# Attention with a gated MLP on one core: 128-query units open their P.V later, their maxima are added by an identity matmul, and one chunk's output is made in two passes

## The chip, the cores and the metric

The kernel runs on one core of one Trainium2 chip. The metric is device time in microseconds (us) of one execution. The engines are PE (TensorE, with PEld for its weight loads), DVE (VectorE), ACT (ScalarE), POOL (GpSimd) and SP (SyncE, which here issues every DMA).

## The reference

The inputs are x [1, 2048, 512], wqkv [512, 1536], wo [512, 512], w1 and w3 [512, 1792], w2 [1792, 512], all bfloat16. Attention has 32 heads of 16 columns.

```python
xn = _layernorm(x)
qkv = (xn @ wqkv).reshape(B, S, 3, H, Dh).transpose(2, 0, 3, 1, 4)
scores = einsum("bhqd,bhkd->bhqk", q, k) * Dh ** -0.5
p = softmax(scores)
o = einsum("bhqk,bhkd->bhqd", p, v).transpose(0, 2, 1, 3).reshape(B, S, D) @ wo
h = silu(x @ w1) * (x @ w3)          # of xn
out = h @ w2
return x + o + out
```

Both branches read the same normalised x; the result is x plus attention plus MLP.

## The kernel before, in words

**Units.** Queries come in 4 chunks of 512 (`qc`), heads in 8 groups of 4 (`g`). A unit is one chunk, one head group and 256 queries; the first two units and the last 16 have 128 queries. There are 73 units, in order of chunk and then group.

**Scores twice.** For each unit the scores are made in two layouts. First with queries on partitions ("p1", L1022), two matmuls of 512 keys into two PSUM banks, which one DVE `tensor_reduce` turns into maxima (L1062, tile `part`): 1,024 of these in all, 16 for a unit of 256 queries and 8 for one of 128. Banks 0 to 3 serve p1, two at a time. Then with keys on partitions ("p2", L1286), one bank at a time out of banks 4 to 7, from which ACT writes exponentials into `PT` (L1299; L1329 does two banks in one instruction, a "pair"): 2,048 banks in all, 32 for a unit of 256 queries and 16 for one of 128. `PT` has 37 slots.

**Maxima into the scores.** The negated maximum of each query has to be in two extra rows of `QT` before p2 of the unit can begin ("AUG"). The final maximum is taken on DVE (L1199) for the first three and the last eight units and by six small POOL instructions for the others (L1170 to L1177); POOL then writes `Z` (L1147, L1149; DVE does it for the last unit). From `Z` there are two ways. In `FAST_AUG` units (the first three, the last eight) PE builds the unit's q afresh from `xnT` with padded weights, four matmuls (for the last two groups of heads with `wq_last`), adds the rows of `Z` through an identity matmul, and ACT moves the result into `QT` (tile "AQ", L797). In all other units SP issues a transposing DMA `Zs<-Z` (L1193) and two DMAs `QT<-Zs` (L1189).

**P.V.** When a unit has at most `PV_LEFT` = 6 exponentials missing, its P.V tile takes one of banks 4 to 7 (L569); ACT copies the result to `U` (L1394), and DMAs and POOL normalise it (L1419, L1439). The last three units (`FAST_PV`) are normalised on DVE instead: a reciprocal (L1384) and a product (L1386), in DVE's queue.

**The rest.** MLP pairs (56, G and U tiles) use the same four banks; ACT evacuates each pair three times (L838, L840, L844) and POOL makes `hT`, which has room for 24 pairs. The output of a chunk (OUT, 4 tiles, PE by the helper line L583, ACT L904) adds x, 14 matmuls with `hT` and 8 with the normalised attention. Its `hT` slots come free when it is done, and only then may later pairs start (`pred_g`). The last chunk has its MLP part first (OUTA, L921) and its attention part added on DVE (OUTB, L935).

**What sets the order.** A greedy planner writes the whole program ahead of time, engine by engine, from costs that it assumes. Every engine then runs its list strictly in order. PE is filled with work of no use ("fill", `xnT,ident` matmuls) where its recent columns fall under a bound:

```python
if recent_cols(c[0]) < RECENT_MIN and c[0] <= end + URG_WAIT:
    return c[0], c[3] if len(c) > 3 else c[1]
```

with 9,400 columns in 2.9 us before. An output is opened by this line, the P.V tile by the next two:

```python
if outs and n >= out_from(NT - 4 - len(outs)) and ok(outs[0]) and exp_unit[min(pv_u[0], NU - 1)] <= OUT_EXP:
left = len(p2_list[u]) - exp_unit[u]
if left > PV_LEFT:
```

Of the kernel before, what the change touches and what calls it, by code (L numbers as in the profile page):

```python
# [215 lines left out]

class _Tile:
# [15 lines left out]
def _c_act(n):  # L233
    return n / 1200.0 + 0.05
# [14 lines left out]
def _build(nc, A_x, A_wqkv, A_wo, B_w1, B_w3, B_w2, out):  # L249
# [12 lines left out]
    NPT = 37  # L262
    NKQ = 2
    NUB = 2
    TOL = 0.0
    PV_LEFT = 6
    ROW_LEAD = 0.45
    PAIR_WAIT = 0.05
    PAIR_DEPTH = 3
    COVER = 0.6  # L270
    MATE = 0.0
    TILE_BANKS = None
    A_LEAD = 0.7
    ROW_LEAD2 = 0.45
    LEAD_AT = 620
    RELAX = 0.06
    PACE = 4500
# [7 lines left out]
    UNIT_TAIL = {i: (128,) * 4 for i in range(1, 5)}  # L285
    DMA_FIRST = 2.95
    DMA_RATE = 360.0
    NFAST = 8
    NPADQ = 2
    NOW = 2  # L290
    WARM_FILL = 12.0
# [9 lines left out]
    OUT_EXP = 14  # L301
# [9 lines left out]
    LOAD_RATE = 5000.0  # L311
    LOAD_CAP = 3000.0
    LOAD_MIN = 3000.0
    RECENT = 2.9
    RECENT_MIN = 9400.0
    URG_WAIT = 0.12
    P2_LOOK = 8
    KEEP = 0.1
    COUPLE = 0.12
# [17 lines left out]
    N_FAST0 = 3  # L337
    FAST_AUG = set(range(N_FAST0)) | set(range(NU - NFAST, NU))
# [8 lines left out]
    with ctx:  # L347
# [18 lines left out]
        wq_last = sb("wq_last", [128, NPADQ, DC * 4 * 32], BF16)  # L366
# [103 lines left out]
        P.op("dve", lambda e: e.memset(wq_last[:, :, :], 0.0), writes=[("wq7",)], occ=0.3 * NPADQ)  # L470
# [60 lines left out]
        def pad(dst, src, g):  # L531
# [4 lines left out]
        padq = {g: wq_last[:, g - NG + NPADQ, :].rearrange("p (a d) -> p a d", d=32)  # L536
                for g in range(NG - NPADQ, NG)}
# [6 lines left out]
        for g in padq:  # L544
            dl, sl_ = pad(padq[g], wq[:, :, :], g)
            poolq["pad"].append(_Item(lambda e, dl=dl, sl_=sl_: e.tensor_scalar(dl, sl_, 1.0, 0.0, ALU.mult, ALU.add),
                                      [("wq",)], [("wq7",)], 0.4, pred=lambda: ("KT", 0, NQC - 1) in done))
        wpad = {("k", 0): wk_first, ("q", 0): wq_first}
        wpad.update({("q", g): padq[g] for g in padq})
# [219 lines left out]
        def qt_groups(qc, g, q0, nq, stop_last):  # L769
            groups = []  # L770
            for c in range(DC):
# [3 lines left out]
                    ([("wq7",)] if g else [("wq0",)] + ON0_KEYS) + xnT_keys(qc * 512 + q0, nq), _c_mm(nq), None))  # L775
# [10 lines left out]
        def tile_QT2(u):  # L786
# [3 lines left out]
            groups = qt_groups(qc, g, q0, nq, False)  # L790
# [20 lines left out]
        def ffn_pair(sc, fc):  # L811
# [35 lines left out]
            def pred_g():  # L847
# [10 lines left out]
                return all(("OUT", (idx - NHT) // FC * 4 + ts) in done for ts in range(4))  # L858
# [16 lines left out]
        def g_h(tg, fc, stop=False):  # L875
# [3 lines left out]
                                          start=False, stop=stop),  # L879
# [13 lines left out]
        def tile_OUT(tg):  # L893
# [4 lines left out]
            def evac(bk):  # L898
                def cb(op):
                    store(tg)  # L900
                    done.add(("OUT", tg))
                    if tg + NXR < NT:
                        load_xr(tg + NXR)
# [1025 lines left out]
```

## Time and profile before

| | us |
|---|---|
| median of 3 runs | 1203.73 |
| the three runs | 1202.17, 1203.73, 1207.64 |
| the profiled execution's own time | 1202.28 |
| its span, first to last instruction | 1200.4 |
| granted TensorE clock, mean | 0.996 |
| busy in the span: DVE / ACT / PE / POOL | 1181.3 / 1169.9 / 1124.1 / 439.3 |

All durations below come from the one profiled execution. Its time stands 1.88 us above its span. A duration on ACT is longer than the step from one instruction to the next, since neighbours overlap by about 0.1 us; steps are taken as the difference of two starts. Line numbers are those of the kernel before; in the kernel after the same statements have other numbers.

### The profile page before, as it was taken

What the parts mean: (1) busy time and instruction counts of PE and PEld (TensorE: products, weight loads), DVE (VectorE), ACT (ScalarE), POOL (GpSimd) and SP (SyncE); (2) the same over time, 40 slices, a digit from 0 to 9 for tenths busy, and PEclk for the clock granted to TensorE, in tenths of its full rate; (3) what the DMA queues carried; (4) which work ended last, traced back from release to release, by engine and by line L of the source; (5) the groups of instructions that cost most, each with busy time, mean ns of one, the idle gap of its engine ahead of it and who ended that gap; (6) DMA issues with size and microseconds to landing.
All of it is one profiled execution on the core that took longest, in us unless ns stands there. A gap on an engine that the chain in (4) does not pass through costs nothing.

```text
span 1200.4 us, 32683 instructions
## 1 busy us (share of the span) xinstructions
PE 1124.1 (94%) x13504; PEld 466.0 (39%) x13660; DVE 1181.3 (98%) x1088; ACT 1169.9 (97%) x2280; POOL 439.3 (37%) x856
## 2 busy tenths in 40 slices
PE   8999999999999999998999999998899999999997
PEld 3433333333334433343333333333333333445554
DVE  9999999999999999999999999999999999999995
ACT  7889999999999999999999999999999999999997
POOL 3254645625222255552222246652222125233220
PEclk9999999999999999998999999999999999999999
DMA  6423223221001121210001122210000111110000
GB/s 188 117 66 82 62 57 76 57 52 41 25 22 33 38 57 42 56 38 19 20 18 31 33 55 59 53 37 20 22 20 24 34 40 24 26 26 19 12 9 25
DMA packets 131248, 52.02 MB, mean 43 GB/s; under 512 B 100140, under 2 KB 131100, under 8 KB 131100
## 3 DMA queue, kind: packets, MB, share of 16 engines
q1 hardware_dynamic: 131100, 49.93, 16.6%
q8 instruction: 107, 1.75, 0.6%
q14 instruction: 41, 0.34, 0.1%
HBM read 38.86 MB, written 6.74 MB: 38 GB/s over the span
## 4 chain that ended last, share of the span: by engine, by line
ACT 38%; PE 34%; DVE 25%; issue 2%; DMA 0%; POOL 0%; ACTq 0%; another core or an unknown queue 0%
ACT PT L1299 29%; DVE part L1062 23%; PE ps L583 13%; PE ps L1286 10%; PE ps L569 6%; ACT PT L1329 5%; PE ps L1022 5%; ACT th L838 1%; ACT zg L840 1%; ACT U L1394 1%; ACT ub L844 1%; ACT kq L745 1%; DVE t L610 1%; DVE hT L643 0%; ACT Vaug L760 0%
## 5 line engine op out<-in xcount | busy, mean ns | idle before, releaser
L1062 DVE TENSOR_REDUCE part<-ps 128x2 f32<-128x1024 f32 x1024 | 1160.2, 1207 | 1.5 <-PE ps L1286 0.7
L1299 ACT ACTIVATE PT<-ps 128x512 bf16<-128x512 f32 x1800 | 944.5, 634 | 5.4 <-PE ps L1286 4.1
L1286 PE MATMUL ps<-QT,KT 32*128 32x256 bf16 (+1 forms) x4672 | 549.4, 259 | 9.9 <-ACT PT L1329 4.3
L1022 PE MATMUL ps<-KT,QT 32*128 32x512 bf16 x2048 | 403.1, 385 | 8.3 <-DVE part L1062 4.0
L1286 PEld LDWEIGHTS ps<-QT,KT 32*128 32x128 bf16 x4672 | 208.1, 92 | 230.2 <-issue 95.9
L1419 POOL TENSOR_TENSOR Rc<-Lc,mone 128x8 f32<-128x8 f32 (+1 forms) x70 | 105.8, 1512 | 268.0 <-DMA Lc<-U 267.9
L583 PE MATMUL ps<-xnT,ident 128*128 128x512 bf16 (+1 forms) x565 | 167.4, 350 | 25.0 <-ACT PT L1329 9.8
L569 PE MATMUL ps<-PT,Vaug 128*17 128x256 bf16 (+1 forms) x4672 | 185.0, 263 | 6.3 <-ACT PT L1299 1.8
L583 PE MATMUL ps<-xnT,w 128*128 128x512 bf16 (+1 forms) x538 | 145.9, 337 | 11.6 <-ACT zg L840 5.0
L1022 PEld LDWEIGHTS ps<-KT,QT 32*128 32x128 bf16 x2048 | 98.6, 91 | 129.9 <-DVE part L1062 73.2
L1329 ACT ACTIVATE PT<-ps 128x1024 bf16<-128x1024 f32 x124 | 127.0, 1056 | 1.7 <-PE ps L1286 1.6
L569 PEld LDWEIGHTS ps<-PT,Vaug 128*17 128x17 bf16 x4672 | 85.7, 89 | 92.0 <-issue 64.7
L583 PEld LDWEIGHTS ps<-xnT,ident 128*128 128x128 bf16 x652 | 48.1, 96 | 106.6 <-ACT PT L1299 54.2
L825 POOL TENSOR_TENSOR a<-zg,ub 128x512 f32<-128x512 bf16 x56 | 64.5, 1152 | 45.8 <-ACT ub L844 45.6
L583 PEld LDWEIGHTS ps<-xnT,w 128*128 128x128 bf16 x566 | 43.1, 97 | 80.4 <-issue 47.4
L827 POOL TENSOR_TENSOR hT<-a,t 128x512 bf16<-128x512 f32 x56 | 70.9, 1266 | 2.5
L583 PE MATMUL ps<-w,hT 128*128 128x256 bf16 (+1 forms) x266 | 68.3, 338 | 2.1 <-issue 1.3
L1170 POOL TENSOR_TENSOR mx<-part 128x16 f32<-128x16 f32 (+1 forms) x62 | 13.1, 211 | 152.6 <-DVE part L1062 152.5
L1439 POOL TENSOR_TENSOR wk_on<-U,R 128x256 bf16<-128x256 f32 (+1 forms) x37 | 23.3, 630 | 92.3 <-DMA R<-rd 92.3
L1439 POOL TENSOR_TENSOR on_b<-U,R 128x256 bf16<-128x256 f32 (+1 forms) x33 | 23.4, 709 | 81.6 <-DMA R<-rd 81.4
L822 POOL TENSOR_SCALAR t<-th 128x512 f32<-128x512 bf16 x56 | 34.7, 619 | 11.5 <-ACT th L838 9.4
L838 ACT ACTIVATE th<-ps 128x512 bf16<-128x512 f32 x56 | 36.0, 642 | 2.3 <-PE ps L583 2.3
(88 smaller groups left out, 509.8 us busy)
## 6 DMA issues: line engine op xcount, KB each, us to landing
w<-in_B_w_dram SPq DMA_DIRECT2D x112, 128.0 KB
R<-rd SPq DMA_DIRECT2D x55, 128.0 KB
QT<-qd SPq DMA_DIRECT2D x31, 128.0 KB
KT<-kd SPq DMA_DIRECT2D x28, 128.0 KB
xr<-in_A_x_dram SPq DMA_DIRECT2D x16, 128.0 KB
out_dram<-osb SPq DMA_DIRECT2D x16, 128.0 KB
qd<-kq SPq DMA_DIRECT2D x15, 128.0 KB
w<-in_B_w_dram SPq DMA_DIRECT2D x1, 1792.0 KB
```

The lines of the kernel that those rows point to most:

```text
L569: ins = e.matmul(bank(bk)[32 * i:32 * i + m, c0 + a:c0 + b], make_lhsT(i), rhs if (a, b) == (0, ncols) else rhs[:, a:b], start=start, stop ...
L583: return e.matmul(bank(bk)[0:rows, c0 + a:c0 + b], lhsT, rhs if (a, b) == (0, ncols) else rhs[:, a:b], start=start, stop=stop, **kw)
L825: q.append(_Item(lambda e: e.tensor_tensor(a32[:, :], zg[:, ss, :], ub[:, ss, :], ALU.mult), [("zg", ss), ("ub", ss)], [("a32",)], 1.1, 1.25))
L827: q.append(_Item(lambda e: e.tensor_tensor(hT[:, hslot(idx), :], a32[:, :], t1[:, :], ALU.mult), [("a32",), ("t1",)], [("hT", hslot(idx))] ...
L838: return [_Item(lambda e: e.activation(th[:, ss, :], bank(bk), ACTF.Tanh, scale=0.5), [("ps", bk)], [("th", ss)], _c_act(512), cb=part_don ...
L1022: ins = e.matmul(bank(2 * sl + i), QT[32 * j:32 * j + 32, qs, q * 128:(q + 1) * 128], KT[32 * j:32 * j + 32, g, c_ * 512:(c_ + 1) * 512], ...
L1062: redq.append(_Item(lambda e: e.tensor_reduce(dst, pair_ap.rearrange("p (a b) -> p a b", b=512), AX.X, ALU.max), writes, [("part", par, qt ...
L1286: ins = e.matmul(bank(b)[:, i * nq:(i + 1) * nq], KT[32 * j:32 * j + 32, g, (k0 + i) * 128:(k0 + i + 1) * 128], QT[32 * j:32 * j + 32, qs, ...
L1299: expq.append(_Item(lambda e: e.activation(PT[:, sl, :], bank(b), ACTF.Exp, scale=SCALE), [("ps", b)], [("PT", sl)], _c_act(512), cb=cb, e ...
L1329: return _Item(lambda e: e.activation(PT[:, s0:s1 + 1:s1 - s0, :], ps8[:, b0:b1 + 1, :], ACTF.Exp, scale=SCALE), [("ps", b0), ("ps", b1)], ...
L1419: poolq["nrm"].append(_Item(lambda e: e.tensor_tensor(Rc[:, pp, 0:nl], Lc[:, pp, 0:nl], mone[:, 0:nl], ALU.pow), [("Lc", pp), ("mone",)], ...
L1439: poolq["nrm"].append(_Item(lambda e: e.tensor_tensor(onorm[ob][:, g, q0:q0 + nq], U[:, us, 0:nq], R[:, pp, 0:nq], ALU.mult), [("U", us)] ...
```

## The change

Six things change together.

1. A unit of 128 queries opens its P.V when 2 exponentials are missing, not 6 (`PV_LEFT_S`).
2. An AQ tile no longer rebuilds q: one identity matmul copies the unit's columns of `QT`, and the rows of `Z` are added as before. So any unit can use it: `FAST_AUG` is now the first 8 units and the last 16. The final maximum stays on DVE for the same eleven units as before (`DVE_MAX`). `wq_last` and what filled it go, and `PT` has 39 slots.
3. The output of chunk 2 has two passes: OUTP makes its 14 `hT` matmuls as soon as its MLP pairs are done and leaves them in `osb`; OUT later adds x, `osb` (through the identity) and the 8 attention matmuls.
4. Later MLP pairs wait for the `hT` part of the earlier output ("HP") instead of the whole output.
5. The bound for fill is 12,800 columns in 3.413 us, of which the last 0.3 us are taken as 1,900 columns per us.
6. Two exponentials may be paired if their banks are neighbours, as before; the constants move into an object `K`, with the same values. `LEADS` is empty and `LEAD2` is 0, so they do nothing.

```diff
-    NPT = 37
+    NPT = 39
+    K = _Lead(ROW_LEAD=0.45, LEAD2=0.0, ANY_PAIR=0, A_LEAD=0.7, RELAX=0.06, KEEP=0.1, PAIR_WAIT=0.05, COVER=0.6, URG_WAIT=0.12, HORIZON=0.3, LOAD_RATE=5000.0, PV_LEFT=6, PV_LEFT_S=2, OUT_EXP=14, PACE=4500, MATE=0.0, COUPLE=0.12)
+    TWO_PASS = (2,)
+    LEADS = {}
...
-    RECENT = 2.9
-    RECENT_MIN = 9400.0
+    CLOCK_W = 3.413
+    CLOCK_MIN = 12800.0
+    ROW_RATE = 1900.0
...
-    FAST_AUG = set(range(N_FAST0)) | set(range(NU - NFAST, NU))
+    FAST_AUG = {u for u in range(NU) if u < FAST_HEAD or u_tr[u] >= FAST_TR}
+    DVE_MAX = {u for u in range(NU) if u < DVE_HEAD or u >= NU - DVE_TAIL}
...
-        P.op("dve", lambda e: e.memset(wq_last[:, :, :], 0.0), writes=[("wq7",)], occ=0.3 * NPADQ)
...
-            groups = qt_groups(qc, g, q0, nq, False)
+            groups = [(lambda bk: all_groups(bk, ident[:, :], QT[:, qs, q0:q0 + nq], nq, stop=False, skip=True),
+                       [("ident",)] + qh_keys(qs, q0, nq), _c_mm(nq), None)]
...
-                return all(("OUT", (idx - NHT) // FC * 4 + ts) in done for ts in range(4))
+                return all(("HP", (idx - NHT) // FC * 4 + ts) in done for ts in range(4))
...
-            groups = [g_x(tg)] + [g_h(tg, fc) for fc in range(FC)]
+            two = qc in TWO_PASS
+            groups = [g_x(tg)] + ([g_b(ts)] if two else [g_h(tg, fc) for fc in range(FC)])
...
+        def g_b(ts):
+            return (lambda bk: all_groups(bk, ident[:, :], osb[:, ts, :], D, start=False, stop=False),
+                    [("ident",), ("osb", ts)], _c_mm(512), None)
+
+        def tile_OUTP(tg):
+            qc, ts = divmod(tg, 4)
+            groups = [g_h(tg, fc, fc == FC - 1, fc == 0) for fc in range(FC)]
+
+            def evac(bk):
+                return [_Item(lambda e: e.activation(osb[:, ts, :], bank(bk), ACTF.Identity),
+                              [("ps", bk)], [("osb", ts)], _c_act(512), cb=lambda op: done.add(("HP", tg)))]
...
-            if u not in FAST_AUG:
+            if u not in DVE_MAX:
                 pool_max()
...
-            if left > PV_LEFT:
+            if left > (K.PV_LEFT if units[u][3] > 128 else K.PV_LEFT_S):
...
+            if parts and ok(parts[0]) and n >= PART_FROM[parts[0].name]:
+                return parts.pop(0)
...
-            if recent_cols(c[0]) < RECENT_MIN and c[0] <= end + URG_WAIT:
+            if recent_cols(c[0], CLOCK_W - K.HORIZON) + ROW_RATE * K.HORIZON < CLOCK_MIN and c[0] <= end + K.URG_WAIT:
```

Since the planner decides again with every one of these, the order moves all along the program. Counted over the whole of it, ACT has 50 single exponentials fewer and 25 pairs more, 8 AQ evacuations of 128 columns and 5 of 256 more, and 4 more copies into `osb`. SP has 39 DMAs fewer (13 transposes, 26 into `QT`). PE has 32 `wq_last` matmuls fewer, 8 of group 0 fewer, 24 of `QT` and 18 of `Z` more, and fill worth 40 more matmuls of 512 columns. DVE loses one memset, and has the following change of order at its end. The names are those of the groups above: `part` and `negm` are maxima, `R` and `wk_on` the reciprocal and normalised attention of the third last unit.

DVE before, from the second last unit's final maximum:

```order
L1199 TENSOR_REDUCE negm<-part 128x4
L1062 TENSOR_REDUCE part<-ps 128x2 x7
L1199 TENSOR_REDUCE negm<-part 128x4
L1147 TENSOR_SCALAR Z<-negm 128x4
L1149 TENSOR_TENSOR Z<-negm,Z 128x4
L1384 RECIPROCAL R<-ps 128x128
L1386 TENSOR_TENSOR wk_on<-ps,R 128x128
```

DVE after, at the same place:

```order
L1216 TENSOR_REDUCE negm<-part 128x4
L1079 TENSOR_REDUCE part<-ps 128x2 x6
L1401 RECIPROCAL R<-ps 128x128
L1403 TENSOR_TENSOR wk_on<-ps,R 128x128
L1079 TENSOR_REDUCE part<-ps 128x2
L1216 TENSOR_REDUCE negm<-part 128x4
L1164 TENSOR_SCALAR Z<-negm 128x4
L1166 TENSOR_TENSOR Z<-negm,Z 128x4
```

The reciprocal and the product of the third last unit have moved ahead of the last maximum of the last unit.

ACT before, from the AQ evacuation of the last unit (the row ahead of these) to the end:

```order
L1329 ACTIVATE PT<-ps 128x1024
L1299 ACTIVATE PT<-ps 128x512 x2
L1329 ACTIVATE PT<-ps 128x2x512
L1299 ACTIVATE PT<-ps 128x512 x2
L1329 ACTIVATE PT<-ps 128x2x512
L1299 ACTIVATE PT<-ps 128x512 x2
L1329 ACTIVATE PT<-ps 128x2x512
L1299 ACTIVATE PT<-ps 128x512 x3
L1329 ACTIVATE PT<-ps 128x2x512
L1299 ACTIVATE PT<-ps 128x512 x3
L1329 ACTIVATE PT<-ps 128x2x512 x2
L1299 ACTIVATE PT<-ps 128x512 x2
```

ACT after, from the same evacuation (its row included) to the end:

```order
L796 ACTIVATE QT<-ps 128x128
L1316 ACTIVATE PT<-ps 128x512
L1346 ACTIVATE PT<-ps 128x2x512
L1316 ACTIVATE PT<-ps 128x512 x2
L1346 ACTIVATE PT<-ps 128x2x512
L1316 ACTIVATE PT<-ps 128x512 x2
L1346 ACTIVATE PT<-ps 128x2x512
L1316 ACTIVATE PT<-ps 128x512 x2
L1346 ACTIVATE PT<-ps 128x2x512 x2
L1316 ACTIVATE PT<-ps 128x512 x2
L1346 ACTIVATE PT<-ps 128x2x512
L1316 ACTIVATE PT<-ps 128x512
```

Behind that evacuation stood 14 single exponentials and 7 pairs; now 10 singles and 6 pairs.

ACT before, behind the last output of chunk 2 (`osb`), with the MLP pairs of chunk 3 that had to wait for it:

```order
L904 ACTIVATE osb<-ps 128x512
L1299 ACTIVATE PT<-ps 128x512 x3
L838 ACTIVATE th<-ps 128x512
L840 ACTIVATE zg<-ps 128x512
L1329 ACTIVATE PT<-ps 128x2x512
L1299 ACTIVATE PT<-ps 128x512 x2
L844 ACTIVATE ub<-ps 128x512
L1299 ACTIVATE PT<-ps 128x512 x8
L1394 ACTIVATE U<-ps 128x256
```

ACT after, behind the same output (`t` is the first OUTA tile of chunk 3):

```order
L905 ACTIVATE osb<-ps 128x512
L1316 ACTIVATE PT<-ps 128x512 x14
L936 ACTIVATE t<-ps 128x512
L1316 ACTIVATE PT<-ps 128x512 x7
L1411 ACTIVATE U<-ps 128x256
L1316 ACTIVATE PT<-ps 128x512 x19
L936 ACTIVATE a<-ps 128x512
```

Four MLP pairs (12 evacuations) stood behind it, one of which is shown; now none does.

More of the change, by code (lines that the diff above doesn't have):

```diff
@@ L901, in cb @@
                     done.add(("OUT", tg))
+                    done.add(("HP", tg))
                     if tg + NXR < NT:
@@ L1624, in note_load, with recent_cols @@
             recent.append((st, w))
-        def recent_cols(st):
-            while recent and recent[0][0] < st - 4.0:
+        def recent_cols(st, span):
+            while recent and recent[0][0] < st - 5.0:
                 recent.pop(0)
-            return sum(w for t, w in recent if t >= st - RECENT)
+            return sum(w for t, w in recent if t >= st - span)
         def low_load(st):
@@ L1703, in pick_pe @@
             if a is not None:
-                late = P.free["dve"] + sum(it.occ for it in redq) - A_LEAD
+                late = P.free["dve"] + sum(it.occ for it in redq) - K.A_LEAD
                 rows.append((max(late, a[2]), a))
```

93 lines of the change are left out of this document (48 added, 45 removed).

## Prediction

> **What bounds the kernel now.** I read the page's busy times first, then the groups, then DVE's waits, then the chain.
>
> ```profile
> PE 1124.1 (94%) x13504; PEld 466.0 (39%) x13660; DVE 1181.3 (98%) x1088; ACT 1169.9 (97%) x2280; POOL 439.3 (37%) x856
> L1062 DVE TENSOR_REDUCE part<-ps 128x2 f32<-128x1024 f32 x1024 | 1160.2, 1207 | 1.5 <-PE ps L1286 0.7
> ```
>
> DVE and ACT are both nearly full. DVE's part is one thing: 1,024 maxima that take 1160.2 us, 1.133 us each, with 1.5 us of idle time ahead of them. The change takes none away, so the end of the maxima can come earlier by 1.5 us at most. DVE's waits for scores (engine, line, released by: total us, times, longest), and the stretches of time in which they lie:
>
> ```profile
> DVE part L1062 <- PE ps L1286: 0.7, 2, 0.5
> DVE part L1062 <- PE ps L1022: 0.6, 1, 0.6
> ...
> 557.00:560.40 3.40, 2.38 (x24) 0.82 (x19) 3.40 (x4) 3.40 (x5) 0.21 (x1) 1.00 0.09 24
> 560.40:563.80 3.40, 2.99 (x35) 0.90 (x39) 3.16 (x4) 2.97 (x5) 2.16 (x9) 0.50 0.06 21
> 563.80:567.20 3.40, 3.40 (x48) 1.27 (x40) 2.45 (x2) 2.33 (x5) 0.00 (x0) 0.50 0.09 19
> ```
>
> In the stretches (us; length; busy PE, PEld, DVE, ACT, POOL; granted clock; DMA) the clock stands at 0.50 from 560.4 to 567.2, after 3.4 us in which PE was busy for 2.38. There DVE loses 0.24 and 0.95 of 3.40, ACT 0.43 and 1.07. So the 1.3 us that DVE waits for scores are this one dip. Then the chain that ended last, in order of time:
>
> ```profile
> 959.30 17.75 DVE part L1062 x16
> 977.47 8.01 DVE part L1062 x7
> 988.22 3.43 ACT PT L1299 x7
> ...
> 1192.15 1.83 ACT PT L1329 x2
> ```
>
> To 985 the chain goes largely through DVE, from 988 to the end through ACT. An exponential needs its unit's maximum, so ACT cannot run ahead of DVE; what counts is how many exponentials are left when the last maximum is done, and whether ACT was idle before. The end itself, DVE then ACT:
>
> ```profile
> 1170.31 8.01 DVE L1062 TENSOR_REDUCE part<-ps 128x2 f32<-128x1024 f32 x7
> 1178.35 0.17 DVE L1199 TENSOR_REDUCE negm<-part 128x4 f32<-128x16 f32 x1
> ...
> 1179.07 0.18 DVE L1149 TENSOR_TENSOR Z<-negm,Z 128x4 bf16<-128x4 f32 x1
> 1179.15 0.95 DVE L1384 RECIPROCAL R<-ps 128x128 f32<-128x128 f32 x1
> 1180.13 0.29 DVE L1386 TENSOR_TENSOR wk_on<-ps,R 128x128 bf16<-128x128 f32 x1
> ...
> 1197.46 0.69 DVE L935 TENSOR_TENSOR osb<-ps,zg 128x512 bf16<-128x512 f32 x1 [0.48 <-remote]
> ...
> 1171.95 0.34 ACT L797 ACTIVATE QT<-ps 128x128 bf16<-128x128 f32 x1
> 1172.11 6.12 ACT L1299 ACTIVATE PT<-ps 128x512 bf16<-128x512 f32 x12
> 1178.78 0.60 ACT L1299 ACTIVATE PT<-ps 128x512 bf16<-128x512 f32 x1 [0.55 <-PE ps L1286]
> 1179.28 1.02 ACT L1329 ACTIVATE PT<-ps 128x1024 bf16<-128x1024 f32 x1
> 1180.18 0.28 ACT L797 ACTIVATE QT<-ps 128x128 bf16<-128x128 f32 x1
> 1180.88 1.02 ACT L1329 ACTIVATE PT<-ps 128x1024 bf16<-128x1024 f32 x1 [0.41 <-PE ps L1286]
> ...
> 1193.84 1.12 ACT L1299 ACTIVATE PT<-ps 128x512 bf16<-128x512 f32 x2
> ```
>
> The last final maximum starts at 1178.35, its AQ evacuation at 1180.18, and ACT then works through 28 exponentials until 1194.96, 5.4 us before the span ends (last P.V groups, reciprocal, output, store).
>
> **The change, part by part.** Steps on ACT from these rows: a single exponential (6.12 - 0.60) / 11 = 0.50 us, a pair 1180.18 - 1179.28 = 0.90, an AQ evacuation of 128 columns 1172.11 - 1171.95 = 0.16. Two more, one for a copy of 512 columns and one for 256 columns (on U, which has the shape of an AQ of 256):
>
> ```profile
> 963.09 0.60 ACT L904 ACTIVATE osb<-ps 128x512 bf16<-128x512 f32 x1
> 963.57 1.11 ACT L1299 ACTIVATE PT<-ps 128x512 bf16<-128x512 f32 x2
> ...
> 1012.19 0.38 ACT L1394 ACTIVATE U<-ps 128x256 f32<-128x256 f32 x1
> 1012.45 1.13 ACT L1299 ACTIVATE PT<-ps 128x512 bf16<-128x512 f32 x2
> ```
>
> that is 0.48 and 0.26. Over the whole program ACT gets 8 x 0.16 + 5 x 0.26 + 4 x 0.48 = 4.5 us more and saves 25 x 0.10 = 2.5 by pairs: 2.0 us more work on an engine that ends the chain.
>
> *Tail.* After the last AQ evacuation 22 exponentials are left instead of 28: 4 singles and a pair fewer, 4 x 0.50 + 0.90 = **-2.9 us**. This holds if DVE is what sets that evacuation.
>
> *DVE's end.* The third last unit's reciprocal and product now stand ahead of the last maximum: 1179.15 to 1180.42, **+1.27 us**. The reciprocal also waits for that unit's P.V, and behind it wait the last maximum, Z, the AQ tile and the last 16 exponentials. PE now issues 13 of the 16 P.V groups between the last two score pairs. I bound this wait by 0 (DVE has a whole maximum, 1.13 us, to cover it) and 0.6 (the longest wait of a maximum for PE above), and take **+0.2**, near the row in which nothing waited.
>
> *Can ACT be there in time?* From 723, the end of ACT's idle time of the first row below, to that evacuation ACT must do more than before: the 2.9 us from the tail, 4 copies for the two passes (1.9), 8 AQ (1.3), less 8 pairs more than before in this stretch (0.8), 5.3 us in all. It was idle there for (700 to 730, then 925 to 1015):
>
> ```profile
> ACT th L838 <- PE ps L583: 1.2, 1, 1.2
> ACT U L1394 <- PE ps L569: 2.0, 3, 1.0
> ACT PT L1299 <- PE ps L1286: 1.1, 2, 0.8
> ACT PT L1329 <- PE ps L1286: 1.0, 1, 1.0
> ```
>
> The last three rows, 4.1 us, are the time of chunk 2's outputs: 23 matmuls a tile keep PE, P.V comes late, and ACT has no MLP evacuations because the last four pairs may not start. With two passes 14 of the 23 are long done (10 are left, the `osb` one included), and the four pairs' 12 evacuations (5.8 us) are done before it too, so ACT carries fewer units' exponentials into this stretch unfinished. I take the 4.1 us as recovered; with the 1.47 us by which DVE ends later, 5.6 are there for 5.3. **0 us**; if none is recovered, +4.1. PE's extra matmuls of the passes and AQ tiles lie in PE's 6% of idle time; what they would cost without it is the second rival.
>
> *Head.* Units 3 to 7 no longer go through DMA. Before, for unit 3:
>
> ```profile
> 77.80 0.23 POOL L1149 TENSOR_TENSOR Z<-negm,Z 128x8 bf16<-128x8 f32 x1
> 78.06 2.27 SPq L1193 DMA_TRANSPOSE Zs<-Z  x1
> 82.12 1.11 SPq L1189 DMA_DIRECT2D QT<-Zs  x2
> 85.36 0.60 ACT L1299 ACTIVATE PT<-ps 128x512 bf16<-128x512 f32 x1 [0.58 <-PE ps L1286]
> ```
>
> Z is done at 78.03 and the first exponential starts at 85.36; for the last unit it took 1180.88 - 1179.25 = 1.6 us by way of PE. So the unit may begin over 5 us earlier. It is worth **0** at the end: DVE is busy throughout, ACT comes down to DVE's pace again by 700 (that is what its wait of 1.2 us for an MLP tile there says), and must then wait that much more. The SP queue has 39 issues fewer, POOL only loses two small ones; neither is on the chain. Two more `PT` slots and the shorter hold of a bank by P.V cost nothing; opening at 2 leaves all 16 P.V groups of the last unit behind its last score, but 12 of them, 0.12 us each by the starts below, fit beside ACT's last two or three instructions: 0, at most +0.3. The memset taken from DVE stands ahead of its wait for x: 0.
>
> ```profile
> 1195.01 0.23 PE L569 MATMUL ps<-PT,Vaug 128*17 128x128 bf16 x4 [1.18 <-ACT PT L1299]
> ...
> 1195.13 0.23 PE L569 MATMUL ps<-PT,Vaug 128*17 128x128 bf16 x4
> ```
>
> *Clock.* The stricter bound asks for about 3,930 columns per us where it was 3,240, and gives 40 more fills. If it prevents the dip, -1.3 us; if dips come at other places, 0. I take half, **-0.65**. [...]
>
> **Sum.** -2.9 + 1.27 + 0.2 + 0 - 0.65 = -2.1 against the profiled execution's own 1202.28: 1200.2. The median of the three runs stands 1.45 above that execution, and I suppose by dips. I carry a little under half of it (0.6): **1200.8**, 0.24% less than 1203.73. About 0.5%, 6.0 us, is what a measurement here can tell from no change: faster means under 1197.7, slower over 1209.75.
>
> **Rivals.**
>
> *ACT becomes the bound.* The 4.1 us of idle time stay (P.V of 256-query units still comes late, U waits) while 5.3 us of work are added: 1204.9. For it: the idle rows say U waits for PE, and PE is no emptier with 40 more fills. Against it: the outputs' 14 matmuls are gone from there.
>
> *PE's fill comes ahead of scores.* Under the bound a fill is issued even where a score pair is due. One matmul of 512 columns takes 0.22 us (five in 1.25, less the last one's 0.38, over four):
>
> ```profile
> 1189.44 1.25 PE L583 MATMUL ps<-wo,wk_on 128*128 128x512 bf16 x5
> ```
>
> A maximum that finds one ahead of its scores without slack starts 0.22 us late, and DVE never makes it up. From 41 of the 1,024 maxima on (9.0 us on 1200.8) it is slower by more than 0.5%; 50 would give 1211.8. Against it: before, with the same rule at a lower bound, DVE lost nothing outside the dip.
>
> *More than the sum.* The dip goes whole (0.65 more), so do the ACT waits of 0.55 and 0.41 us at the tail, the 0.2 for P.V, DVE's wait of 0.48 for the last output and the runs' surplus: 1200.2 - 2.3 = 1197.9, and the shorter AQ tile (two matmuls for five) a little less, some 1197.5. For it: the AQ tile, P.V and the output there were all made over. Against it: each wait has to go.
>
> *The orders hold, but nothing moves*: dip elsewhere, the reciprocal waits its 0.6, P.V at the end 0.3: 1202.28 - 2.9 + 1.27 + 0.6 + 0.3 = 1201.6, or 1202.2 with the 0.6 of the runs, inside the forecast's own range.
>
> **Chances.** Forecast, 1199 to 1203: 0.50. ACT the bound, 1203 to 1207: 0.20. Fill ahead of scores, over 1209.75: 0.14. More than the sum, under 1197.7: 0.16. The range leaves out the fill and the lower part of the last: 1197.0 to 1207.0. Faster 0.16, within 0.70, slower 0.14.
>
> **What would show it.** Right: the DVE waits for `part` near nothing and no stretch of clock 0.50 before the end; ACT idle near 80 gone and more of it before 700; ACT's waits for U at the time of chunk 2's outputs gone; last AQ evacuation near 1179 to 1181 and 22 exponentials behind it, ACT's end near 1192.5. Wrong: waits of maxima for L1022's successor spread over the program; several dips; an ACT that reaches the last AQ tile late, so that the tile has stood finished in PSUM.

## The result and the profile after

| | before | after |
|---|---|---|
| median of 12 runs, us | 1204.08 | 1199.65 |
| lowest and highest | 1202.17, 1209.48 | 1198.94, 1201.14 |
| ratio, with its 95% interval | | 0.996 [0.9948, 0.9972] |
| the profiled execution's own time | 1202.28 | 1199.56 |
| its span | 1200.4 | 1197.8 |

The kernel is 0.4% faster, and its runs lie within 2.2 us of each other where those of before lay within 7.3. The page of after, busy times, the chain's shares by engine and the group of the maxima:

```profile
PE 1116.0 (93%) x13564; PEld 467.9 (39%) x13731; DVE 1180.1 (99%) x1087; ACT 1174.2 (98%) x2272; POOL 439.9 (37%) x854
...
DVE 44%; ACT 27%; PE 25%; issue 3%; POOL 1%; DMA 1%; another core or an unknown queue 0%; POOLq 0%
...
L1079 DVE TENSOR_REDUCE part<-ps 128x2 f32<-128x1024 f32 x1024 | 1159.9, 1212 | 0.7 <-PE ps L1303 0.4
```

DVE's maxima stay what they were, their idle time falls from 1.5 to 0.7 us, and the chain goes through DVE more than through any other engine. At the time of the old clock dip (columns as in the prediction's table of stretches) the clock is now whole and DVE loses nothing:

```profile
557.00:560.40 3.40, 3.02 (x29) 0.94 (x30) 3.40 (x4) 3.40 (x8) 0.85 (x2) 1.00 0.11 39
560.40:567.20 6.80, 6.47 (x110) 2.81 (x112) 6.80 (x7) 6.78 (x14) 1.57 (x8) 1.00 0.12 32
```

The end of after, DVE first, then ACT (start, duration, engine, line, operation; in brackets the wait ahead of it):

```profile
1169.05 6.87 DVE L1079 TENSOR_REDUCE part<-ps 128x2 f32<-128x1024 f32 x6
1176.57 0.96 DVE L1401 RECIPROCAL R<-ps 128x128 f32<-128x128 f32 x1 [0.66 <-PE ps L567]
1177.57 0.29 DVE L1403 TENSOR_TENSOR wk_on<-ps,R 128x128 bf16<-128x128 f32 x1
1177.78 1.21 DVE L1079 TENSOR_REDUCE part<-ps 128x2 f32<-128x1024 f32 x1
1179.02 0.17 DVE L1216 TENSOR_REDUCE negm<-part 128x4 f32<-128x16 f32 x1
...
1180.90 0.27 ACT L796 ACTIVATE QT<-ps 128x128 bf16<-128x128 f32 x1
...
1191.54 0.60 ACT L1316 ACTIVATE PT<-ps 128x512 bf16<-128x512 f32 x1
```

Between the two profiled executions the 2.72 us are made up so:

| step | us |
|---|---|
| the second last unit's maxima are done earlier (1170.31 to 1169.05) | -1.26 |
| reciprocal and product ahead of the last maximum | +1.27 |
| the reciprocal's wait for P.V | +0.66 |
| from the final maximum to the AQ evacuation | +0.05 |
| from there to ACT's end (14.78 to 11.24) | -3.54 |
| ACT's end to the span's end, and outside the span | +0.10 |

The first row is a sum. Counted by the starts of the maxima (one every 1.13 us where nothing holds DVE up), the dip of before had delayed DVE by 1.9 us, more than the 1.3 us of idle time that the prediction read, and smaller waits by some 0.2. Against that stand 0.8 us of waits that before has not, at 1054, 1073 and 1080 us; where the largest of them comes from is shown with f3.

These two executions differ by 2.7 us, the medians by 4.4. The rest lies in the runs. Each run has a mean granted clock beside its time, and over 74 runs of the kernel before, made beside the experiments, the two go together: the three runs with a clock of 0.999 took 1200.15, 1200.22 and 1200.33 us, those with 0.995 took 1202.7 to 1204.8, those with 0.989 up to 1207.5. A straight line through the 29 runs of one chip falls by 5.95 us for each 0.01 of clock, through 25 runs of another by 7.3, through 20 of a third by 8.1. A dip of 6.8 us at half clock takes 0.0028 from the mean, so one costs about 1.7 to 2.3 us, which fits the 1.9 above, and the median run of before (0.995 or 0.996) has one or two of them. Of the 12 runs of after ten stand at 0.999 or 1.0, with a median of 1199.47. So without dips the change is worth about 0.8 us (1200.2 to 1199.5); the other 3.6 of the 4.4 us are dips that no longer come. The 1200.2 rests on three runs only, but the two profiled executions give the same: 1202.28 less the 1.9 us of its dip is 1200.4, 0.8 above 1199.56.

### The profile page after: what moved, and what is told of

The parts are those of the page before. It is cut to its first block, busy times and chain, and to the rows that moved or that the text cites. A ratio compares the mean times of both kernels' runs of the same rounds, so it can differ in the third digit from the quotient of the medians.

```text
span 1197.8 us, 32744 instructions
## 1 busy us (share of the span) xinstructions
PE 1116.0 (93%) x13564; PEld 467.9 (39%) x13731; DVE 1180.1 (99%) x1087; ACT 1174.2 (98%) x2272; POOL 439.9 (37%) x854
## 4 chain that ended last, share of the span: by engine, by line
DVE 44%; ACT 27%; PE 25%; issue 3%; POOL 1%; DMA 1%; another core or an unknown queue 0%; POOLq 0%
DVE part L1079 43%; ACT PT L1316 19%; PE ps L581 9%; PE ps L1303 7%; PE ps L567 5%; PE ps L1037 4%; ACT PT L1346 3%; ACT th L837 1%; ACT zg L839 1%; ACT ub L843 1%; ACT U L1411 1%; ACT xnT L672 0%; ACT kq L743 0%; ACT Vaug L758 0%; DMA R<-rd 0%
## 5 line engine op out<-in xcount | busy, mean ns | idle before, releaser
L1316 ACT ACTIVATE PT<-ps 128x512 bf16<-128x512 f32 x1750 | 922.4, 627 | 5.7 <-PE ps L1303 2.5
L1303 PE MATMUL ps<-QT,KT 32*128 32x256 bf16 (+1 forms) x4672 | 538.0, 259 | 11.7 <-ACT PT L1346 6.0
L1303 PEld LDWEIGHTS ps<-QT,KT 32*128 32x128 bf16 x4672 | 204.3, 92 | 224.8 <-issue 96.9
L581 PE MATMUL ps<-xnT,ident 128*128 128x512 bf16 (+1 forms) x599 | 174.6, 348 | 23.0 <-ACT PT L1346 7.0
L567 PE MATMUL ps<-PT,Vaug 128*17 128x256 bf16 (+1 forms) x4672 | 175.2, 261 | 4.5 <-ACT zg L839 1.3
L1346 ACT ACTIVATE PT<-ps 128x1024 bf16<-128x1024 f32 x149 | 151.7, 1050 | 0.8 <-PE ps L1303 0.5
L581 PEld LDWEIGHTS ps<-xnT,ident 128*128 128x128 bf16 x700 | 52.3, 97 | 107.7 <-ACT PT L1316 47.7
L839 ACT ACTIVATE zg<-ps 128x512 bf16<-128x512 f32 x56 | 36.3, 649 | 0.0
L843 ACT ACTIVATE ub<-ps 128x512 bf16<-128x512 f32 x56 | 35.9, 641 | 0.0
```

What stands on the lines that cost most here:

```text
L567: ins = e.matmul(bank(bk)[32 * i:32 * i + m, c0 + a:c0 + b], make_lhsT(i), rhs if (a, b) == (0, ncols) else rhs[:, a:b], start=start, stop ...
L581: return e.matmul(bank(bk)[0:rows, c0 + a:c0 + b], lhsT, rhs if (a, b) == (0, ncols) else rhs[:, a:b], start=start, stop=stop, **kw)
L839: _Item(lambda e: e.activation(zg[:, ss, :], bank(bk), ACTF.Identity, scale=0.5), [("ps", bk)], [("zg", ss)], _c_act(512), cb=part_done, n ...
L843: return [_Item(lambda e: e.activation(ub[:, ss, :], bank(bk), ACTF.Identity), [("ps", bk)], [("ub", ss)], _c_act(512), cb=part_done)]
L1303: ins = e.matmul(bank(b)[:, i * nq:(i + 1) * nq], KT[32 * j:32 * j + 32, g, (k0 + i) * 128:(k0 + i + 1) * 128], QT[32 * j:32 * j + 32, qs, ...
L1316: expq.append(_Item(lambda e: e.activation(PT[:, sl, :], bank(b), ACTF.Exp, scale=SCALE), [("ps", b)], [("PT", sl)], _c_act(512), cb=cb, e ...
```

## The experiments

All twelve at a glance. "Clean" runs are those with a clock of 0.999 or more, and their median is taken as the kernel's time without dips. This is not exact: a single dip of 3.4 us takes 0.0014 from the mean, and the fall of the clock at the very end of the program takes some too (in after it stands at 0.50 for the last 2.04 us of the span, 0.0009 by the same sum), so a run at 0.999 can hold one short dip (the profiled run of g4 does, at 21.1 us). How many runs are clean is a result too. The kernels of one letter ran on one chip, beside the same runs of before (medians 1204.60 with e, 1202.64 with f, 1202.82 with g). Most expectations missed: only f4's theory has the measured median in its range, g4's lies 0.07 under its range, e1's lies in its rival's, and the other nine lie in no range that was named.

| kernel | what it is | median, us | ratio to before, 95% | clean runs, their median |
|---|---|---|---|---|
| before | | see above | | 3 of 74, 1200.2 |
| after | | 1199.65 | 0.996 [0.9948, 0.9972] | 10 of 12, 1199.47 |
| e1 | after, output of chunk 2 in one pass | 1199.93 | 0.996 [0.9948, 0.9973] | 6 of 6, 1199.93 |
| e2 | after, old bound for fill | 1205.02 | 0.9998 [0.9982, 1.0014] | 4 of 12, 1200.60 |
| e3 | after, P.V at 6 missing | 1204.09 | 0.9999 [0.9986, 1.0011] | 1 of 12, 1201.78 |
| e4 | before, new bound | 1203.47 | 0.9997 [0.9984, 1.0010] | 8 of 12, 1202.65 |
| f1 | after, fill a quarter as wide | 1203.43 | 1.0021 [1.0001, 1.0041] | 7 of 12, 1203.25 |
| f2 | after, reciprocal behind last maximum | 1200.50 | 0.9986 [0.9966, 1.0005] | 8 of 12, 1200.12 |
| f3 | after, AQ only for the last 8 units of the tail | 1196.62 | 0.9945 [0.9931, 0.9959] | 6 of 6, 1196.62 |
| f4 | after, AQ only for the first 3 units of the head | 1199.30 | 0.9969 [0.9957, 0.9982] | 8 of 8, 1199.30 |
| g1 | before, new bound and P.V at 2 | 1201.99 | 0.9993 [0.9982, 1.0004] | 8 of 11, 1201.74 |
| g2 | f3 with one pass | 1200.28 | 0.9979 [0.9970, 0.9988] | 8 of 10, 1200.03 |
| g3 | f3 with the late reciprocal | 1197.46 | 0.9953 [0.9939, 0.9966] | 5 of 5, 1197.46 |
| g4 | after with 37 slots | 1198.93 | 0.9964 [0.9951, 0.9976] | 5 of 5, 1198.93 |

**What takes the dips away: e2, e3, e4, g1.** The first puts the old bound back, the second the old opening of P.V.

```diff
-    K = _Lead(..., HORIZON=0.3, ...)
+    K = _Lead(..., HORIZON=0.0, ...)
...
-    CLOCK_W = 3.413
-    CLOCK_MIN = 12800.0
+    CLOCK_W = 2.9
+    CLOCK_MIN = 9400.0
```

> The changed kernel with the old bound for fill (9,400 columns in 2.9 us). Its order has as many fills as the changed one (600 against 598), placed elsewhere, and 19 exponentials behind the last AQ evacuation instead of 22. Theory A (a clock dip costs 1.3 us each and the bound prevents it): the single runs scatter over 4 us or more as those of the kernel before did (1202.2 to 1209.5), the profile has at least one stretch at clock 0.50 before the end, the median is 1200 to 1202.5, one or two dips less a tail shorter by 1.5. Rival B (the bound prevents nothing, dips come by chance): 1198 to 1199.7, with the scatter of the changed kernel (2.2 us). Rival C (the whole gain is the bound): 1203 to 1205.

```diff
-    K = _Lead(..., PV_LEFT_S=2, ...)
+    K = _Lead(..., PV_LEFT_S=6, ...)
```

> The changed kernel with P.V of 128-query units opened at 6 missing exponentials again. In its order 27 exponentials stand behind the last AQ evacuation instead of 22 and the reciprocal stands behind the last maximum. Theory: 5 exponentials more, +2.5 us, and the reciprocal's 1.27 and its wait of 0.66 gone from ahead of the last maximum, -1.9: 1199.9 to 1200.8. Rival (a P.V tile that holds one of the four banks longer starves ACT all through the last 16 units): ACT waits for scores between 1030 and 1180 rise by over 1 us, 1201 to 1203. Rival (opening late only delays): 1198 to 1199.

Each of the two alone gives the whole gain back: both are level with the kernel before. In their profiles the dip is there again, at other places. The stretches (length; busy PE, PEld, DVE, ACT, POOL; granted clock; DMA), e2 first:

```profile
1078.10:1081.50 3.40, 2.47 (x66) 1.43 (x60) 3.40 (x4) 2.80 (x4) 1.17 (x4) 0.99 0.02 1
1081.50:1088.30 6.80, 6.80 (x81) 2.87 (x79) 5.26 (x5) 4.81 (x11) 2.02 (x6) 0.50 0.05 12
```

and e3:

```profile
997.50:1000.90 3.40, 2.37 (x28) 0.78 (x25) 3.40 (x4) 3.40 (x6) 1.26 (x3) 1.00 0.11 21
1000.90:1004.30 3.40, 3.40 (x19) 0.90 (x20) 2.63 (x3) 1.94 (x4) 0.68 (x1) 0.50 0.03 2
```

DVE loses 1.54 of 6.8 us in the one and 0.77 of 3.4 in the other, about the fifth of a dip that it lost before (1.19 of 6.8); by the starts of the maxima it is more, as told in the last section. But e2 without dips (1200.60) is only 1.1 us from after, so what the old bound costs is mostly dips; e3's one clean run is still 2.3 us above after. Its DVE waits for scores late in the program, in small pieces (1.14 us in these five), and 27 exponentials are left behind its last AQ evacuation where after has 22. The DVE rows:

```profile
1078.75 31.79 DVE L1079 TENSOR_REDUCE part<-ps 128x2 f32<-128x1024 f32 x28 [0.20 <-PE ps L1303]
1110.73 1.23 DVE L1079 TENSOR_REDUCE part<-ps 128x2 f32<-128x1024 f32 x1 [0.19 <-PE ps L1303]
1112.31 4.62 DVE L1079 TENSOR_REDUCE part<-ps 128x2 f32<-128x1024 f32 x4 [0.35 <-PE ps L1037]
...
1163.26 9.14 DVE L1079 TENSOR_REDUCE part<-ps 128x2 f32<-128x1024 f32 x8 [0.23 <-PE ps L1303]
...
1178.30 2.36 DVE L1079 TENSOR_REDUCE part<-ps 128x2 f32<-128x1024 f32 x2 [0.17 <-PE ps L1037]
```

The other way round, the two parts were put into the kernel before, the bound alone (e4), and both (g1, whose second line is shown):

```diff
-    RECENT = 2.9
-    RECENT_MIN = 9400.0
+    RECENT = 3.113
+    RECENT_MIN = 12800.0
...
-            if recent_cols(c[0]) < RECENT_MIN and c[0] <= end + URG_WAIT:
+            if recent_cols(c[0]) + 1900.0 * 0.3 < RECENT_MIN and c[0] <= end + URG_WAIT:
```

> The kernel before with the new bound for fill alone. Its order has 562 fills against 558, and 27 exponentials behind the last AQ evacuation against 28. Theory A (the bound prevents dips): no clock 0.50 before the end, the runs scatter by 2 to 3 us in place of 7, median 1201.0 to 1202.2. Rival B (the bound prevents nothing): 1203.5 to 1204.5 and a scatter like that of the kernel before. Rival C (the whole gain is the bound): 1199.5 to 1200.5.

```diff
...
-            if left > PV_LEFT:
+            if left > (PV_LEFT if units[u][3] > 128 else 2):
```

> The kernel before with two parts of the change alone: the new bound for fill and P.V of 128-query units opened at 2 missing exponentials. 29 exponentials stand behind the last AQ evacuation (28 before), the reciprocal behind the last maximum as before. Theory A (these two together keep the clock up, which is most of the gain; each alone did not): granted clocks of 0.998 or more in nearly all runs, scatter under 2.5 us, 1200.0 to 1201.5. Rival B (dips are a matter of chance of each order): some runs at clock 0.996 or lower and a scatter of over 4 us, 1202 to 1204.5.

The bound alone makes 8 of 12 runs clean instead of 3 of 74, and costs 2.4 us in them (1200.2 to 1202.65), so its median is where before's is: fill in front of work is paid for, by about as much as the dips cost. Some 1.4 us of the 2.4 stand in the starts of e4's maxima, which, the dip of before left aside, fall behind its maxima in pieces of 0.1 to 0.4 us. P.V at 2 beside it takes 0.9 off again and leaves 8 of 11 clean (the other three lose 0.002 to 0.003). From g1 to after it is another 2.3 us, by what is left of the change: AQ, two passes, slots.

Since every kernel has an order of its own, dips could be a matter of chance of the order. The runs speak against it: over the nine kernels that have both parts (f1 left out) 64 of 75 runs are clean, over the two with the old bound (before, e2) 7 of 86. With the new bound and P.V at 6 it is 8 of 12 (e4) and 1 of 12 (e3), so for the later P.V the case is weaker.

**Is it the share of the array? f1.** The planner counts a matmul's columns by the share of the array that it uses. In f1 a fill writes 32 partitions instead of 128, in the same order of work.

```diff
+        def quarter(bk, n):
+            return all_groups(bk, ident[:, 0:32], xnT[:, 0, 0:n], n, rows=32)
...
-                P.pe(all_groups(bk, ident[:, :], xnT[:, 0, 0:512], 512),
+                P.pe(quarter(bk, 512),
...
-                P.pe(all_groups(bk, ident[:, :], xnT[:, 0, 0:256], 256),
+                P.pe(quarter(bk, 256),
```

> The changed kernel with the same order on every engine, in which each fill matmul writes 32 partitions in place of 128, so that it uses a quarter of the array for the same number of columns. PE is busy for the same time; no result of the kernel changes. Theory A (the clock falls where the share of the array that was used in 3.4 us is low, whatever PE's busy time): stretches at clock 0.50 all through the parts without MLP work (fill is 24 to 30 matmuls of 512 columns per 18 us there), ten or more of them, each some 2 us: 1215 to 1300. Theory B (only idle time of PE counts): no dips, 1199.3 to 1200, as the changed kernel.

Seven of twelve runs are clean and five show a clock of 0.990 to 0.994 (1208 to 1211 us); the profile caught one of the five:

```profile
1073.20:1076.60 3.40, 2.50 (x31) 1.19 (x30) 3.30 (x3) 2.99 (x7) 2.31 (x8) 1.00 0.01 0
1076.60:1090.30 13.70, 13.17 (x168) 6.78 (x169) 9.52 (x8) 9.40 (x16) 3.55 (x11) 0.50 0.05 11
```

One long dip or none is neither what theory A nor what theory B forecast: by A some 700 fills count a quarter and dips should come all along the program. So the width of the fill did not decide it here, and it is not shown to count for nothing. The clean runs are 3.8 us above those of after. The profile shows where: from 60 to 1000 us, ahead of the dip, f1's maxima fall behind those of f2 (the same fills at full width, and no dip) by 3.0 us, in pieces of 0.2 us or less. Why narrow fill makes them late isn't shown; it isn't free here.

**The end of DVE: f2 and g3.** The third last unit's reciprocal and product are held until the last score pair's maximum is in DVE's queue, in after and (g3) in f3.

```diff
+        held_fin = []
...
+                if p1_n[0] >= NP1:
+                    redq.extend(held_fin)
+                    del held_fin[:]
...
-                        redq.extend(items)
+                        (redq if p1_n[0] >= NP1 else held_fin).extend(items)
```

> The changed kernel with the third last unit's reciprocal and product held back until the last maximum is in DVE's queue; all else by the same rules. 24 exponentials (10 singles, 7 pairs) stand behind the last AQ evacuation instead of 22. Theory (DVE sets that evacuation): the 1.27 and the wait of 0.66 go from ahead of the last maximum, one pair of 0.9 is added: 1198.5 to 1199.2, and the last final maximum starts at 1177.1 instead of 1179.0. Rival (ACT is the bound there and only its wait of 0.95 at 1176.3 can go): 1199.2 to 1199.8.

> The changed kernel with AQ tiles for the last 8 units only, and the third last unit's reciprocal and product held back until the last maximum is in DVE's queue. 18 exponentials (10 singles, 4 pairs) stand behind the last AQ evacuation. Theory (DVE sets the end there, nothing waits for P.V ahead of the reciprocal): the last final maximum 1.2 us earlier, 1195.2 to 1196.0. Rival (PE holds the last scores back behind the P.V groups, as in the run with 16 AQ tiles, where DVE waited 1.29 for them; or ACT is the bound): 1196.2 to 1196.9.

Neither gains. DVE in f2:

```profile
1168.87 6.87 DVE L1080 TENSOR_REDUCE part<-ps 128x2 f32<-128x1024 f32 x6
1177.03 1.23 DVE L1080 TENSOR_REDUCE part<-ps 128x2 f32<-128x1024 f32 x1 [1.29 <-PE ps L1307]
1178.29 0.17 DVE L1220 TENSOR_REDUCE negm<-part 128x4 f32<-128x16 f32 x1
```

PE still has its P.V groups ahead of the last scores, so the last maximum waits 1.29 us for these: the 1.27 us of the reciprocal had stood in time that DVE would have waited anyway. The final maximum comes 0.73 us earlier (1178.29 for 1179.02), and 24 exponentials are left behind the AQ tile instead of 22. What the prediction counted as +1.27 is real in the sum, but it can't be had back by moving the reciprocal alone.

In g3 DVE waits for nothing, and its last final maximum is 0.87 us earlier than f3's (1176.81 for 1177.68). Yet the AQ evacuation comes 0.64 later (1180.00 for 1179.36): PE starts the AQ tile only at 1179.37, behind other scores and output matmuls, though DVE had finished `Z` at 1177.40. So there it is PE's order, and no longer DVE, that sets the end.

**AQ tiles in the tail: f3.** Only the last eight units take the identity way; the eight before them go through DMA again.

```diff
-    FAST_TR = 896
+    FAST_TR = 960
```

> The changed kernel with only the last 8 units by AQ tile, as before; the 8 units ahead of them go by the transposing DMA again. 18 exponentials (12 singles, 3 pairs) stand behind the last AQ evacuation instead of 22. Theory (AQ tiles of those 8 units cost ACT 1.3 us and buy nothing, since the exponentials lag their maxima by more than the DMA way takes): 1197.5 to 1198.7 without dips. Rival (the DMA way makes ACT wait between 1030 and 1110): ACT's waits for scores there rise by 2 us or more, 1200.5 to 1203.

This is the fastest kernel measured, 0.9945 of before, and its highest run (1197.61) lies under the lowest of f4 (1198.42), which ran beside it and differs little from after. Its end, DVE and ACT:

```profile
1175.24 0.94 DVE L1401 RECIPROCAL R<-ps 128x128 f32<-128x128 f32 x1
1176.22 0.29 DVE L1403 TENSOR_TENSOR wk_on<-ps,R 128x128 bf16<-128x128 f32 x1
...
1177.68 0.17 DVE L1216 TENSOR_REDUCE negm<-part 128x4 f32<-128x16 f32 x1
...
1179.36 0.27 ACT L796 ACTIVATE QT<-ps 128x128 bf16<-128x128 f32 x1
...
1186.50 2.27 ACT L1316 ACTIVATE PT<-ps 128x512 bf16<-128x512 f32 x4
```

The reciprocal waits for nothing (0.66 in after), the AQ evacuation is 1.54 us earlier, and 18 exponentials are left instead of 22. From there to ACT's end it takes 9.41 us instead of 11.24. Where ACT's time comes from, the groups of pairs and AQ evacuations, after first:

```profile
L1346 ACT ACTIVATE PT<-ps 128x1024 bf16<-128x1024 f32 x149 | 151.7, 1050 | 0.8 <-PE ps L1303 0.5
...
L796 ACT ACTIVATE QT<-ps 128x128 bf16<-128x128 f32 (+1 forms) x24 | 7.7, 319 | 0.9 <-PE ps L581 0.7
```

and f3:

```profile
L1346 ACT ACTIVATE PT<-ps 128x1024 bf16<-128x1024 f32 x162 | 164.4, 1051 | 0.9 <-PE ps L1303 0.5
...
L796 ACT ACTIVATE QT<-ps 128x128 bf16<-128x128 f32 (+1 forms) x16 | 5.4, 335 | 0.6 <-PE ps L581 0.5
```

Eight evacuations fewer (8 x 0.16 = 1.3 us) and 13 pairs more (13 x 0.10 = 1.3 us). Up to 1015 us the two kernels have the same exponentials and pairs (101 pairs each), so the change of the tail made the difference. A likely reason is that an AQ tile takes one of the four banks where a pair needs two; this was not tested by itself.

The tail's AQ tiles also cost DVE time. In after PE stands at such a tile until POOL has written `Z`, and the scores behind it come late:

```profile
1072.16 0.23 PE L581 MATMUL ps<-ident,Z 128*128 128x128 bf16 x1 [0.68 <-POOL Z L1166]
...
1073.29 2.36 DVE L1079 TENSOR_REDUCE part<-ps 128x2 f32<-128x1024 f32 x2 [0.40 <-PE ps L1303]
```

This is the largest of the three waits named with the result (0.48 of 0.8 us by the starts of the maxima); f3 has none of the three. So the 2.9 us between after and f3 lie in the last final maximum, 1.34 us earlier, and in four exponentials fewer behind it, 1.83 us.

**Two passes: e1 and g2.** Chunk 2's output in one pass, in after and in f3.

```diff
-    TWO_PASS = (2,)
+    TWO_PASS = ()
```

> The changed kernel with the output of chunk 2 in one pass again (later MLP pairs wait for the whole output). In its order 26 exponentials stand behind the last AQ evacuation instead of 22, and the third last unit's reciprocal stands behind the last maximum again. My theory (DVE sets the last maximum, the tail is what ACT has left): the waits of ACT for PE at chunk 2's outputs come back (3 to 4 us between 925 and 1015), so ACT is late at the end; 2.0 us more tail, 1.9 us less on DVE ahead of the last maximum, and 1 to 3 us of ACT that is not recovered: 1201 to 1203, against 1199.65 for the changed kernel. Rival, the two passes are worth nothing and the gain is the clock bound: 1199.5 to 1200, with ACT as busy from 925 to 1015 as in the changed kernel.

> The changed kernel with AQ tiles for the last 8 units only and the output of chunk 2 in one pass. 23 exponentials (13 singles, 5 pairs) stand behind the last AQ evacuation against 18 with two passes. Theory (with less AQ work DVE sets the end, and what is left behind the last maximum is what two passes change): 5 exponentials or 2.3 us more than 1196.62: 1198.4 to 1199.4, and ACT waits of 1 to 2 us between 945 and 975. Rival (two passes are worth 0.3 as they were with 16 AQ tiles): 1196.7 to 1197.3.

In after it hardly matters (1199.93 for 1199.47 in clean runs), in f3 it costs 3.4 us. ACT's waits from 925 to 1015 are 4.1 us before, 0.4 after and, in e1:

```profile
ACT PT L1346 <- PE ps L1303: 0.6, 1, 0.6
ACT PT L1316 <- PE ps L1303: 0.6, 1, 0.6
ACT U L1411 <- PE ps L567: 0.5, 1, 0.5
```

So 2.4 of the 4.1 us went without the two passes, and these bring the other 1.3 for 4 copies (1.9 us) and 18 pairs fewer (149 for e1's 167, 1.8 us). In g2 the same 1.7 us of waits stand there, but the last final maximum comes at 1179.70 instead of f3's 1177.68 (1.05 of it by a dip that its profiled run has at 824 us), and 23 exponentials are left at the end instead of 18, which is 2.5 us. In e1 the planner also put the reciprocal behind the last maximum (final maximum at 1177.07, not 1179.02), which makes up for its 26 exponentials. The gains of the parts don't add: AQ in the tail and one pass cost 2.9 and 3.4 us singly, and 3.3 together.

**Head and slots: f4 and g4.**

```diff
-    FAST_HEAD = 8
+    FAST_HEAD = 3
```

> The changed kernel with units 3 to 7 by the transposing DMA again. 23 exponentials (15 singles, 4 pairs) stand behind the last AQ evacuation and the reciprocal behind the last maximum. Theory (what ACT gains at the head is lost by 700): ACT's waits of 4 us between 78 and 86 are back, and the time of a run without dips is 1198.5 to 1200. Rival (the head's gain lasts): 1203 to 1204. Dips, which any order may bring, would show as scatter of over 3 us and granted clocks below 0.998, and add to either.

```diff
-    NPT = 39
+    NPT = 37
```

> The changed kernel with 37 slots for exponentials in place of 39. 19 exponentials (13 singles, 3 pairs) stand behind the last AQ evacuation against 22, with 10 pairs fewer in the whole program. Theory (two slots cost and bring nothing): the last AQ evacuation comes later by what ACT has to do before it, the end within 0.7 of 1199.65: 1199.0 to 1200.4, scatter under 2.5 us. Rival (late P.V needs the slots; ACT waits for scores because p2 waits for a slot): ACT's waits for scores between 1030 and 1180 rise by over 1 us, 1200.8 to 1203.

Neither costs anything. In f4 ACT waits near 80 again as it did before (4.5 us from 76 to 88):

```profile
ACT ub L843 <- PE ps L581: 2.4, 2, 1.3
ACT th L837 <- PE ps L581: 0.9, 1, 0.9
ACT PT L1316 <- PE ps L1303: 0.7, 1, 0.7
ACT U L1411 <- PE ps L567: 0.5, 1, 0.5
```

where after has 1.1 us:

```profile
ACT PT L1316 <- PE ps L1303: 0.6, 1, 0.6
ACT U L1411 <- PE ps L567: 0.5, 1, 0.5
```

and yet f4 is not slower. It makes 168 pairs where after makes 149 (86 against 70 between 90 and 700 us), and has five evacuations of 256 columns fewer: 1.9 + 1.3 us of work that stands against the 3.4 us of waits.

## Why the prediction was right, and where its terms were off

The forecast was 1200.8 within 1197 to 1207, and "within 0.5%" had 0.70; it came to 1199.65, 0.37% below before. The likeliest case is the one that came. Its mechanism holds, but its terms were off in opposite directions, and that the sum came so near is in part luck: the work gained 0.6 us less than forecast and the dips 2.1 us more.

- *Tail, -2.9:* right. 22 exponentials stand behind the last AQ evacuation, and ACT needs 3.54 us less; the 0.6 beyond the sum are waits that went from there, the 0.41 quoted in the prediction among them.
- *DVE's end, +1.27 and +0.2:* the order did what was counted, to 0.01 us. The wait for P.V was 0.66, just above the upper bound of 0.6. I had taken the lower part of the range because DVE has a whole maximum to cover it; it does not cover 13 P.V groups that PE puts ahead of the last scores. f2 shows that the same 13 groups delay the scores by about as much if the reciprocal is out of the way.
- *ACT in time, 0:* right in its outcome, or nearly: the last AQ tile was finished on PE at 1180.35 and evacuated at 1180.90, behind a pair (before, 1180.03 and 1180.18). The step that failed is its working. The 4.1 us of waits did go, but e1 shows 2.4 of them going without the two passes. And the AQ tiles were costed at their evacuations alone, 1.3 us; f3 shows 2.9 us for those in the tail: 13 pairs go with them, PE's wait for `Z` makes DVE late, and the reciprocal waits. The prediction had put PE's part in PE's idle time, at nothing. That its 5.6 met its 5.3 was a balance of wrong entries, and luck.
- *Head, 0:* right (f4). The prediction said that ACT would have to wait more before 700 instead; it does not (0.4 us from 90 to 700, 1.5 before). The time went into pairs that f4 makes and after does not, not into waits.
- *Clock, -0.65, and +0.6 for the runs:* this is the term that was mis-sized. I took one dip of the profiled run as the measure, read it as 1.3 us of idle time where the starts of the maxima give 1.9, took half of the 1.3, and let the 1.45 us between that run and the median stand as unexplained. The runs show 2.4 to 4.4 us of dips in the median run of before (1202.64 and 1204.60 against 1200.2), and nearly none in after. That the stricter fill keeps the dip away was an estimate of mine, put at one half; the runs speak for it: with the old bound (e2) eight of twelve runs have dips and with the new one (after) two of twelve. None of the six traces with a dip has a gap of PE longer than 0.72 us in the 3.4 us ahead of it.
- *The rival of fill ahead of scores* had a small part in after (its maxima keep the pace of before until 1050 us, but for the dip; behind that the waits at 1054 and 1080, 0.3 us together, have fills ahead of their scores), but it is a true cost: e4 pays 2.4 us for the bound when P.V still opens at 6. That it came out even in after rests on the other parts.
- *ACT the bound* fell, in after. In g2 it is part of what happens: 2.5 us of exponentials more are left, beside a later last maximum.

Of the 2.9 us that I had forecast from median to median, 1.43 were work and 1.5 dips (0.65, and 0.85 of the runs' 1.45); of the 4.4 that came, 0.8 are work and 3.6 dips.

What stays open: why P.V at 6 brings dips under the new bound (e3), why narrow fill makes the maxima late (f1), whether the bank is what costs the pairs (f3), and why the parts' gains don't add. Every one of these changes lets the planner order all the work anew, and a difference of 0.5 us between two kernels may be no more than that.

## What to carry to other kernels

Where the runs of a kernel scatter, set each run's time against its own granted clock before forecasting anything: the intercept is the kernel, the slope is the dips (5.95 to 8.1 us for each 0.01 of clock here), and a change may be worth more in the second than in the first. Cost a tile that is added to a full pipeline also by what its matmuls wait for in PE's order (0.68 us for `Z` in after) and by the pairs that go with it (13 in f3's comparison), and not only by its own evacuation. Measure a stall on a full engine by how late its next instructions start, not by its idle time (1.9 us against 1.3 here). And try the parts of a combined change one at a time on top of the whole: here the one that was left out, AQ in the tail, had been giving back nearly three of the six microseconds, dips included, that the rest gains.

## What the runs showed of the hardware

**The clock fell without a long idle gap.** In the 3.4 us ahead of a dip PE had no matmul for 0.93 us in all (e2), 1.03 (e3) and 0.90 (f1), and the longest gap between matmuls was 0.51, 0.52 and 0.72. In before the first record of a clock of 1.00 starts at 7.408 us; the clock falls to 0.50 at 560.367, rises to 1.00 at 567.194 and falls to 0.50 at 1198.659. In after the first record starts at 7.923 and the clock falls at 1195.761. Within each of these two traces these times lie whole multiples of 3.4133 us apart, to 0.003 us: in before the dip starts 162.000 of them after the first record and lasts 2.000. Why they do, and why the same kernel has dips in one run and none in the next, is not shown.

**What brings a dip is not shown.** In the stretch ahead of a dip PE was busy for 2.37 to 2.50 of 3.40 us (e2, e3, f1 above). Only traces with as many matmul records as weight loads are used for this; those of before and after lack 156 and 167 (13504 for 13660, 13564 for 13731), so the 2.38 us of before in the prediction may be too low. But stretches as low go by without a dip, in e2 itself and in f3 (two lines):

```profile
1047.30:1050.70 3.40, 2.27 (x29) 0.76 (x28) 3.40 (x4) 3.40 (x5) 1.31 (x5) 1.00 0.11 39
304.50:307.90 3.40, 2.48 (x27) 0.86 (x26) 3.40 (x5) 3.40 (x6) 2.38 (x5) 1.00 0.04 4
997.50:1000.90 3.40, 2.37 (x29) 0.77 (x26) 3.40 (x4) 3.40 (x5) 1.65 (x1) 1.00 0.11 21
```

The last has nearly the counts of e3's stretch at the same time, which was followed by a dip. Neither PE's busy time nor the planner's columns by array share (f1) tells these stretches apart from those ahead of a dip.

**The dips here cost more than a quarter of their length.** By busy time DVE, on which everything hangs here, lost 0.77 of 3.4 us (e3), 1.19 and 1.54 of 6.8 (before, e2) and 4.18 of 13.7 (f1). By the starts of its maxima, which is what the rest of the program sees, they came 1.3 us late in e3, 1.9 in before, 2.4 in e2 and some 5 in f1: 0.28 to 0.4 of the dip.
